# A gated linear-attention layer with a gated MLP: operand loads issued in two halves at two places of the cycle

## The chip, the cores and the metric

The kernel runs on one core of one Trainium2 chip. The metric is the device time of one execution in microseconds (us), lower is better. PE is TensorE with its matmuls, PEld its weight loads, DVE is VectorE, ACT ScalarE, POOL GpSimd, and SP (SPq in rows) the queue that issues every DMA of this kernel.

## The reference

The first half is a recurrence over 768 steps for 4 batches and 8 heads of 40 channels; its output, laid out as 320 channels per step, goes through a gated MLP.

```python
for t in range(S):                       # S = 768
    y[:, :, t] = einsum('bhd,bhde->bhe', r_t, state)
    Sa = einsum('bhde,bhe->bhd', state, a_t)
    state = state * w_t[:, :, None, :] - einsum('bhd,bhe->bhde', Sa, b_t)
    state = state + einsum('bhd,bhe->bhde', v_t, k_t)
x = y.transpose(0, 2, 1, 3).reshape(B, S, 320)
h = gelu_tanh(x @ w_in)                  # 320 -> 1024
u, v = h[..., :512], h[..., 512:]
v_n = (v - mean(v)) / sqrt(var(v) + 1e-6) * g_ln
v_s = einsum('ts,bsd->btd', w_sg, v_n) + b_sg
out = x + (u * v_s) @ w_out
```

## The kernel before, in words

The recurrence is cut into 12 chunks of 64 steps (`NCH`, index `c`), and the 4 batches into two pairs (index `f`). One pass over a chunk for both `f` is called a cycle here. Per `(c, f)` there are two strings of pieces. The *gate* pieces (`gate_1` to `gate_n`) turn the operands w, k, a, b of a chunk into decayed keys (`kb`, transposed to `kbt`) and 64x64 blocks (`ab`); they run several chunks ahead. The *chain* pieces (`chain1` to `chain5` on PE, with their `post` pieces on ACT and DVE) carry the state from chunk to chunk. In between, the inverse of a triangular matrix is built, most of it on POOL (`inv_sub`, tile names `tg` and `x`), and parts of the MLP (`fill_x`, `fill_v`, `fill_out`, tiles `xf`, `hf`, `hv`) are put into the cycles from chunk 2 on. The rest of the MLP follows the attention.

Every piece has a position, a number in units of a plan (one cycle is 25.258 units, `PER`). The pieces are sorted by position and written out in that order, and each engine runs its own instructions in exactly this order. A position is an order, not a time: what stands behind a waiting instruction on the same engine waits too. That holds for SP as well.

The pieces that matter here issue DMAs on SP:

- `load_main` (L274) fills one of two tiles `main` with the operands w, k, a, b of the chunk pair `2c+f+2`, in two DMAs: 40 channel rows into partitions 0 to 39 and 40 rows into partitions 64 to 103. It stands at `y + n[5] + LATE` (L663), behind the second `gate_3`, the last reader of the tile. The next reader is `gate_1` of the following cycle.
- `load_rv` (L492) fills `rts[f]` and `vuts[f]` with r and v for the next chunk in four DMAs, two for each half `x` of the partitions. It stands at `z + n[13] + LATE` (L670), behind `chain5`, and is next read by `chain4` of the following cycle.
- `store5` (L628) writes the chunk's output in four DMAs (`xd<-yt`), `load_vb` (L481) loads v in another layout (`vs<-vb`), `fill_x` loads earlier outputs again (three DMAs, `xf<-xd`), and `fill_out` stores a piece of the MLP (`hd<-hv`).

With the positions of the file, SP meets in a cycle, for `f` = 0 and 1 as marked: `vs` (0), `xf`, `rv` (1), `store5` (1), `hd`, `main` (0), `vs` (1), `xf`, `rv` (0), `main` (1), `store5` (0), `hd`. On PE a cycle is, by tile names: hf, kt, gp, pq, ru, xp, tp, yp, us, hf, ut, ab, kt, ru, pq, us, sp, ut, yp, ab.

Of the kernel before, what the change touches and what calls it, by code (L numbers as in the profile page):

```python
# [16 lines left out]
B, H, S, D = 4, 8, 768, 40  # L17
# [23 lines left out]
LOADS = -12.0  # L41
PER = 25.258
LATE = 2.5
STORE = 1.5
GATE = ((-101.908, -100.107, -99.028, -96.184, -97.801, -95.604, -92.188, -90.251, -93.577, -91.478, -91.823),
    (-93.163, -92.271, -89.673, -85.987, -88.462, -85.151, -80.147, -78.616, -83.325, -79.712, -81.287))
GATE0 = {(0, 0): (-50.0, (0, 0.6, 1.2, 2.0, 2.1, 3.5, 5.0, 6.2, 6.1, 10.6, 7.4)), (0, 1): (-43.168, (-2.368, -1.768,
# [159 lines left out]
def engines(tc):  # L207
    nc = tc.nc
    return tuple(InOrder(tc, e) for e in (nc.vector, nc.scalar, nc.gpsimd, nc.tensor, nc.sync))
# [6 lines left out]
def attention(tc, a, xd, flag, keep, ps, mlp=None):  # L216
# [3 lines left out]
    V, A, G, T, Q = engines(tc)  # L220
    with ExitStack() as ctx:
# [20 lines left out]
        def static(nm, n, shape, where=None):  # L242
            return [(where or st).tile(shape, F32, name=f"{nm}{i}") for i in range(n)]
# [11 lines left out]
        n = WU  # L255
# [7 lines left out]
        rts = static("rt", 2, [128, 2, 4, C])  # L263
        call = keep.tile([128, NCH * B, NP], F32, name="call")
        vuts = static("vut", 2, [128, 2, 2, 4, C])
# [5 lines left out]
        def main_of(i):  # L271
            return mains[i % 2]

        def load_main(i):  # L274
            if i < 2 * NCH:
                for h in range(2):
                    Q.dma_start(out=main_of(i)[64 * h:64 * h + D], in_=a["main"][i, D * h:D * h + D])

        warm = gt.tile([128, 128], F32, name="warm")
        V.memset(warm, 0.0)  # L280
# [208 lines left out]
                A.copy(out=vus[f][0:64, 0:2 * DM].rearrange("p (g h x d) -> p g h x d", g=4, h=2, x=2),  # L489
                       in_=vss[f][0:64].rearrange("p i (g x) h d -> p (i g) h x d", x=2))  # L490

        def load_rv(c, f):  # L492
            if c < NCH:
                for x in range(2):
                    r = slice(64 * x, 64 * x + D)
                    Q.dma_start(out=rts[f][r], in_=a["rt"][c, f, x])
                    Q.dma_start(out=vuts[f][r, 0], in_=a["vt"][c, f, x])

        def chain1(c, f):
            at, vs = at_of(c, f), vss[f]  # L500
# [138 lines left out]
        def at_(p, f, *args, **kw):  # L639
            pieces.append((p, f, args, kw))  # L640
# [4 lines left out]
            at_(ZEROS + 0.01 * k, f)  # L645
        for f in range(2):
            at_(LOADS, load_vb, 0, f)
            at_(LOADS, load_rv, 0, f)
        for c in range(NCH):
            for f in range(2):  # L650
                y, n = GATE0.get((c, f)) or (YG[c], GATE[f])
                at_(y + n[0], gate_1, c, f, 0)
                at_(y + n[1], gate_1, c, f, 1)
                at_(y + n[2], gate_2, c, f, E={"V": V, "G": G}[GATEE.get((c, f), GE)[0]])
                at_(y + n[3], gate_c, c, f)
                for i in range(2):
                    at_(y + n[4 + i], gate_3, c, f, i, E={"V": V, "G": G}[GATEE.get((c, f), GE)[1]])
                for g, p in zip((gate_t, gate_k, gate_s), n[6:]):
                    at_(y + p, g, c, f)
                for h in range(2):  # L660
                    at_(y + n[9] + 0.001 * h, gate_a, c, f, h)
                    at_(y + n[10] + 0.001 * h, gate_n, c, f, h)
                at_(y + n[5] + LATE, load_main, 2 * c + f + 2)  # L663
                z, n = YC[c], CHAIN0.get((c, f), CHAIN[f])
                for g, p in zip((chain1, post1, chain_t, post_t, chain2, post2, chain3, post3, copy3, chain_u, post_u, chain4, post4, chain5, post5), n):
                    at_(z + p, g, c, f)
                at_(z + n[14] + STORE, store5, c, f)
                at_(z + n[0] + LATE, load_vb, c + 1, f)
                at_(z + max(n[6], n[9]) + LATE, load_vu, c + 1, f)
                at_(z + n[13] + LATE, load_rv, c + 1, f)  # L670
            z = YC[c]
            for (g, *k), p in zip(((inv_back, 0), (inv_back, 1), (inv_back, 2), (inv_g,), (post_g,), (inv_x,), (post_x,)), BACK0.get(c, BACK)):
                at_(z + p, g, c, *k)
        for g in GROUPS:
            z, v = (0, INV0[g[0]]) if g[0] in INV0 else (YC[g[0]], INV)
            at_(z + v[0], inv_load, g)
            at_(z + v[1], inv_in, g)
            for s in range(31 - LAST):
                y = {}
# [523 lines left out]
def attention_then_gated_mlp(tc, ins, out):  # L1203
    nc = tc.nc
    a = ins
    with ExitStack() as ctx:
        keep = ctx.enter_context(tc.tile_pool(name="keep", bufs=1))
        dr = ctx.enter_context(tc.tile_pool(name="x_dram", bufs=1, space=bass.MemoryType.DRAM))
        xd = dr.tile([B, DM, S], F32, name="xd")
        flag = keep.tile([1, 1], I32, name="flag")  # L1210
        mlp = [a[k] for k in ("w_in", "w2", "g_ln", "wst", "b_sg", "w_out", "seq_w")]
        ps = Banks(tc, ctx)
        part = Mlp(tc, ps, xd, *mlp, out)
        part.hd = dr.tile([B, LASTF, 128, HF], F32, name="hd")
        verdict = attention(tc, a, xd, flag, keep, ps, part)
        part.run(True, verdict)
        bad = nc.values_load(flag, min_val=0, max_val=1)
        with tc.If(bad > 0):
            sequential(tc, [a["seq_" + k] for k in "rkvwab"], xd)
            Mlp(tc, ps, xd, *mlp, out).run(False)  # L1220
# [60 lines left out]
```

## Time and profile before

| | |
|---|---|
| time, median of 3 runs | 648.37 us (646.72 to 649.48) |
| the profiled execution's own time | 651.27 us |
| its span, first to last instruction | 649.5 us |
| PE / DVE / ACT / POOL busy | 85% / 77% / 56% / 57% of the span |
| mean granted TensorE clock | 0.899 of full speed |
| chain that ended last | PE 46%, DVE 26%, issue 10%, POOL 7%, ACT 6%, DMA 2% |

The profile is one execution; its own time is what the shares and stretches belong to. The chain that ended last is followed back from the last instruction to what released each step. "issue" in it is time in which an engine waited for nothing that the profile shows. [...] DMA shares are of 16 DMA engines.

### The profile page before, as it was taken

The page shows a single profiled execution, that of the slowest core. Times are in us where ns is not written, and L with a number is a line of the kernel's source. Part 1 is how long each engine was busy: PE and PEld are TensorE (multiplying, and loading weights), DVE is VectorE, ACT ScalarE, POOL GpSimd, SP SyncE. Part 2 cuts the span into 40 slices and gives each one's busy share as a digit, 9 for nine tenths or more (in the row PEclk, how much of TensorE's full clock was granted, in tenths as well). Part 3 has the DMA queues.
Part 4 walks back from the last instruction along what each step waited for, and adds up shares of the span by engine and source line. Part 5 has one row for each costly group of instructions (what it writes and reads, how often), then busy time and mean ns, then how long its engine had stood idle before and what let it go on. Part 6 is the DMA issues. An engine that isn't in the chain of part 4 may idle for free.

```text
span 649.5 us, 25246 instructions
## 1 busy us (share of the span) xinstructions
PE 551.1 (85%) x10734; PEld 502.6 (77%) x10734; DVE 496.9 (77%) x954; ACT 363.6 (56%) x769; POOL 370.0 (57%) x600
## 2 busy tenths in 40 slices
PE   6438859768998798999998799698998998899896
PEld 5327758657887787888887687597998987899896
DVE  7767989699779566877799856748699799778943
ACT  3333957457877576787867678556345324625410
POOL 3485838816974844588389642656644632544331
PEclk8658877567999897999998899788999999999999
DMA  5443334243444353553354346337023541401001
GB/s 194 130 120 94 96 80 117 77 121 89 128 113 134 91 151 92 154 131 108 105 137 134 106 133 168 106 113 203 14 80 104 157 144 67 124 26 56 30 13 55
DMA packets 54945, 69.69 MB, mean 107 GB/s; under 512 B 21704, under 2 KB 39752, under 8 KB 52808
## 3 DMA queue, kind: packets, MB, share of 16 engines
q1 hardware_dynamic: 54824, 67.99, 36.8%
q8 instruction: 86, 1.41, 1.0%
q14 instruction: 35, 0.29, 0.1%
HBM read 54.86 MB, written 13.11 MB: 105 GB/s over the span
## 4 chain that ended last, share of the span: by engine, by line
PE 46%; DVE 26%; issue 10%; POOL 7%; ACT 6%; DMA 2%; SPq 1%; DVEq 0%; POOLq 0%; ACTq 0%
PE sg L202 7%; PE yp L202 5%; PE hf L202 4%; PE op L202 3%; DVE v L202 3%; PE sp L202 3%; PE ab L202 3%; PE pq L202 3%; PE ut L202 3%; PE ru L202 3%; DVE stg L202 3%; PE hu L202 3%; PE kt L202 2%; PE xp L202 2%; DVE p L202 2%
## 5 line engine op out<-in xcount | busy, mean ns | idle before, releaser
L202 POOL TENSOR_TENSOR tg<-x,n 128x135 f32<-128x135 f32 (+25 forms) x203 | 106.2, 523 | 98.1 <-ACT gs L202 40.0
L202 POOL TENSOR_TENSOR x<-x,tg 128x135 f32<-128x135 f32 (+25 forms) x203 | 108.2, 533 | 15.9
L202 PE MATMUL sg<-wsh,vh 128*128 128x384 f32 x192 | 65.9, 343 | 4.6 <-DVE y L202 3.9
L202 PE MATMUL sg<-wsh,vl 128*128 128x384 f32 x192 | 66.0, 344 | 3.5 <-POOL vl L202 3.5
L202 PE MATMUL sg<-wsl,vh 128*128 128x384 f32 x192 | 65.8, 343 | 1.7 <-DVE wsl L202 0.9
L202 ACT ACTIVATE nts<-ab 32x512 f32<-32x512 f32 x96 | 46.5, 484 | 28.2 <-PE ab L202 27.0
L202 PE MATMUL kt<-ident,kb 128*128 128x128 f32 x192 | 35.4, 333 | 27.4 <-DVE fixed L202 17.8
L202 POOL TENSOR_TENSOR gx<-g,gy 128x384 fp32r<-128x384 f32 x30 | 32.0, 1076 | 40.1 <-ACT gy L202 40.1
L202 PEld LDWEIGHTS kt<-ident,kb 128*128 128x128 f32 x192 | 26.7, 170 | 32.6 <-issue 26.7
L202 DVE TENSOR_TENSOR at<-ab,mask 64x512 f32<-64x512 f32 x48 | 31.8, 677 | 26.1 <-ACT nts L202 25.4
L202 POOL TENSOR_TENSOR rs<-rs,mhalf 128x1 f32<-128x1 f32 x24 | 14.7, 615 | 64.9 <-DVE rs L202 61.3
L202 ACT CAST vh<-v 128x512 fp32r<-128x512 f32 x24 | 14.6, 620 | 58.3 <-DVE v L202 58.3
L202 PE MATMUL ab<-at,kb 64*64 64x64 f32 x1536 | 39.6, 269 | 7.1 <-DVE fixed L202 6.2
L202 PEld LDWEIGHTS ab<-at,kb 64*64 64x64 f32 x1536 | 35.7, 179 | 10.1 <-issue 8.4
L202 ACT CAST gy<-g 128x384 fp32r<-128x384 f32 x30 | 15.3, 513 | 50.2 <-DVE g L202 50.2
L202 PEld LDWEIGHTS sg<-wsh,vh 128*128 128x128 f32 x192 | 36.5, 190 | 5.9 <-issue 2.6
L202 PEld LDWEIGHTS sg<-wsh,vl 128*128 128x128 f32 x192 | 36.6, 191 | 5.4 <-POOL vl L202 5.4
L202 PE MATMUL yp<-pqs,kbt 128*64 128x64 f32 x768 | 33.5, 249 | 7.8 <-ACT vs L202 3.4
L202 PEld LDWEIGHTS yp<-pqs,kbt 128*64 128x64 f32 x768 | 29.5, 159 | 11.6 <-ACT vs L202 3.6
L202 PEld LDWEIGHTS sg<-wsl,vh 128*128 128x128 f32 x192 | 36.5, 190 | 2.3 <-DVE wsl L202 1.2
L202 PE MATMUL sp<-vu,kbt 128*64 128x40 f32 x704 | 28.1, 237 | 11.6 <-issue 8.7
L202 DVE SCALAR_TENSOR_TENSOR g<-sg,gl,bt 128x384 f32<-128x384 f32 x32 | 19.5, 610 | 23.9 <-POOL gx L202 14.9
(158 smaller groups left out, 1609.2 us busy)
## 6 DMA issues: line engine op xcount, KB each, us to landing
main<-main SPq DMA_DIRECT2D x44, 321.4 KB
hd<-hv SPq DMA_DIRECT2D x20, 256.0 KB
v<-hd SPq DMA_DIRECT2D x20, 256.0 KB
vs<-vb SPq DMA_DIRECT2D x24, 160.0 KB
rt<-rt SPq DMA_DIRECT2D x48, 80.0 KB
vut<-vt SPq DMA_DIRECT2D x48, 80.0 KB
xd<-yt SPq DMA_DIRECT2D x96, 40.0 KB
ws<-seq_w SPq DMA_DIRECT2D x20, 192.0 KB
```

The source lines that it names most:

```text
L202: return self.tc.keep_in_program_order(f(*a, **k))
```

## The change

The two DMAs of `load_main` become two pieces, and the four of `load_rv` become two pieces of two. The first half stays where it was. The second half of `main` moves later by 4.6 units for `f` = 0 and 3.4 for `f` = 1, from chunk `c` = 2 on; the second half of r and v moves later by 1.7 and 1.15 units, for all chunks. Bytes, shapes and number of DMAs stay.

```diff
+MAIN_GAP = (4.6, 3.4)
+RV_GAP = (1.7, 1.15)
...
-        def load_main(i):
+        def load_main(i, h):
             if i < 2 * NCH:
-                for h in range(2):
-                    Q.dma_start(out=main_of(i)[64 * h:64 * h + D], in_=a["main"][i, D * h:D * h + D])
+                Q.dma_start(out=main_of(i)[64 * h:64 * h + D], in_=a["main"][i, D * h:D * h + D])
...
-        def load_rv(c, f):
+        def load_rv(c, f, x):
             if c < NCH:
-                for x in range(2):
-                    r = slice(64 * x, 64 * x + D)
-                    Q.dma_start(out=rts[f][r], in_=a["rt"][c, f, x])
-                    Q.dma_start(out=vuts[f][r, 0], in_=a["vt"][c, f, x])
+                r = slice(64 * x, 64 * x + D)
+                Q.dma_start(out=rts[f][r], in_=a["rt"][c, f, x])
+                Q.dma_start(out=vuts[f][r, 0], in_=a["vt"][c, f, x])
...
-            at_(LOADS, load_rv, 0, f)
+            for x in range(2):
+                at_(LOADS, load_rv, 0, f, x)
...
-                at_(y + n[5] + LATE, load_main, 2 * c + f + 2)
+                for h in range(2):
+                    at_(y + n[5] + LATE + (MAIN_GAP[f] if h and c > 1 else 0), load_main, 2 * c + f + 2, h)
...
-                at_(z + n[13] + LATE, load_rv, c + 1, f)
+                for x in range(2):
+                    at_(z + n[13] + LATE + (RV_GAP[f] if x else 0), load_rv, c + 1, f, x)
```

## Rows read from the trace of the kernel before

**Rows 1.** The page, parts 1, 3 and 6: engines, queues, DMA issues.

```profile
PE 551.1 (85%) x10734; PEld 502.6 (77%) x10734; DVE 496.9 (77%) x954; ACT 363.6 (56%) x769; POOL 370.0 (57%) x600
...
q8 instruction: 86, 1.41, 1.0%
...
main<-main SPq DMA_DIRECT2D x44, 321.4 KB
```

**Rows 2.** Busy time by stretch: us, engines, granted clock, DMA share, GB/s.

```profile
90.00:115.00 25.00, 21.01 (x602) 19.17 (x603) 24.55 (x44) 15.95 (x36) 18.33 (x33) 0.69 0.42 111
...
156.60:221.40 64.80, 57.52 (x1891) 51.49 (x1883) 51.11 (x95) 50.03 (x109) 49.27 (x85) 1.00 0.49 129
221.40:228.20 6.80, 6.60 (x161) 6.29 (x161) 2.36 (x5) 1.31 (x2) 6.09 (x10) 0.50 0.05 14
...
252.20:259.00 6.80, 6.80 (x163) 6.42 (x162) 4.38 (x12) 2.35 (x5) 0.00 (x0) 0.50 0.06 18
```

**Rows 3.** The chain that ended last: start us, us, what.

```profile
115.13 1.52 issue
...
168.02 2.05 PE hf L202 x8
...
191.25 1.08 PE ut L202 x32
192.32 1.67 PE yp L202 x64
...
194.93 2.05 PE hf L202 x8
...
200.08 1.88 issue
...
217.82 3.78 issue
...
221.93 1.90 PE ut L202 x32
223.83 2.93 PE yp L202 x64
...
228.43 2.05 PE hf L202 x8
...
248.17 2.54 issue
...
258.83 2.14 PE hf L202 x8
...
276.74 1.09 PE pq L202 x64
```

**Rows 4.** Timeline of SP, 195 to 260 us: start us, us, what.

```profile
195.54 0.66 SPq L202 DMA_DIRECT2D main<-main  x2
...
212.96 0.71 SPq L202 DMA_DIRECT2D main<-main  x2
213.84 0.48 SPq L202 DMA_DIRECT2D vs<-vb  x1
...
228.30 0.66 SPq L202 DMA_DIRECT2D main<-main  x2
...
242.88 0.71 SPq L202 DMA_DIRECT2D main<-main  x2
...
245.81 0.47 SPq L202 DMA_DIRECT2D vs<-vb  x1
...
257.15 0.29 SPq L202 DMA_DIRECT2D rt<-rt  x1
```

**Rows 5.** Busy time in a stretch with little but one `main` pair moving.

```profile
157.50:161.50 4.00, 4.00 (x147) 3.72 (x144) 3.01 (x7) 3.74 (x9) 3.61 (x6) 1.00 0.54 150
```

**Rows 6.** Timeline of DVE, 240 to 242.5 us: the next reader of a `main` tile.

```profile
241.44 1.27 DVE L202 TENSOR_TENSOR_SCAN ex<-main,fixed 128x260 f32<-128x260 f32 x2
```

**Rows 7.** Timeline of POOL, 150 to 430 us; in brackets idle time before, and releaser.

```profile
264.89 0.24 POOL L202 TENSOR_TENSOR tg<-x,n 128x31 f32<-128x31 f32 x1 [12.80 <-ACT gs L202]
```

## The prediction

> **What bounds the kernel now.** I read the busy time by stretch first, then the chain that ended last, then the SP timeline beside both. From about 156 to 286 us the chain is an almost unbroken string of PE matmuls, so what PE loses there the kernel loses. A cycle from `hf` to `hf` takes 26.91 us (168.02 to 194.93), then 33.50 (to 228.43), then 30.40 (to 258.83) [rows 3]. The two long cycles hold the two longest "issue" pieces, 3.78 us at 217.82 and 2.54 us at 248.17, in which PE waited for nothing that the profile names [rows 3]. Behind each, the granted clock is 0.50 for 6.80 us, while it was 1.00 from 156.6 to 221.4, through the shorter stop of 1.88 us at 200.08 [rows 2, 3].
>
> What is PE waiting for? The page has a queue of kind "instruction" with 86 packets in 1.41 MB, 16.4 KB each; PE and PEld have 21,468 instructions, 250 for each packet [rows 1]. So I take these packets for PE's program, and a stop without a releaser for a packet that came late. The stops follow the `main` pairs: 212.96 and 217.82 (4.9 us later), 242.88 and 248.17 (5.3), 195.54 and 200.08 (4.5) [rows 3, 4]. A pair is 2 x 321.4 = 643 KB [rows 1]; where hardly anything else moved, the rate was 150 GB/s [rows 5], so a pair drains in about 4.29 us and a half in 2.14, an estimate. My reading: a program packet asked for while a pair is in the DMA queues comes only behind all of it.
>
> [...]
>
> **The change part by part.** No DMA is added and none gets smaller, so SP's issue time stays. What changes is what SP has between two halves.
>
> *Second half of main, f = 0.* The position moves by 4.6 units past one piece, `load_vb` of f = 1, and stays ahead of `fill_x`. A position alone makes no pause; `vs` does, since it waits for PE's `ru`. After the pair at 242.88, `vs` went out at 245.81, so the second half comes about 3.4 us behind the first, past the 2.14 us that the first needs. After the pair at 212.96, `vs` went out at 213.84, so the second half comes at about 214.4, only 1.4 us behind the first [rows 4]. There a packet gets between the halves only if it was asked for in that time. Queued behind the moved half is `xf`, as before.
>
> In both cycles I take it that the packet now waits for one half, not two. The stop of 3.78 becomes 3.78 - 2.14 = 1.64 us and that of 2.54 becomes 0.40. Both are shorter than the 1.88 us after which the clock stayed at 1.00 [rows 2, 3], so the half-clock stretches go too. Their price: `ut` took 1.90 us instead of 1.08 and `yp` 2.93 instead of 1.67 [rows 3], 1.755 times as long. PE's 6.60 busy us in the first stretch [rows 2] are then 3.76 at full clock, 2.84 lost; the 6.80 of the second are 3.87, 2.93 lost. Gains: 2.14 + 2.84 = 4.98 and 2.14 + 2.93 = 5.07, together 10.05 us. The other way round: the two cycles are longer than the one at 168.02 by 6.59 and 3.49, together 10.08, which that sum may take but hardly exceed unless the common cycle shortens as well.
>
> *Second half of main, f = 1.* It moves by 3.4 units behind the four stores, the second r and v piece and `hd`. It then drains in the stretch gp, pq, ru, xp, tp, yp, where PE uses instructions fastest: `pq`, 64 matmuls and 64 loads, takes 1.09 us [rows 3], so a packet of 250 lasts 2.13 us there. A half of 2.14 us in the way is as long as that whole packet. For the first half the same sum as above applies: the stop of 1.88 at 200.08 may go. Between a gain of 1.88 and a loss of 2.14 for each of the five or so cycles from 156 to 286, I take nothing, and keep -1.9 and +10.7 as the ends.
>
> *Is the later half still in time?* The tightest pair I found is that at 228.30, whose reader starts at 241.44 [rows 4, 6]: 13.1 us, less 4.3 for the drain of both, leaves 8.8. The new place costs three to four, so nothing. If the cover were gone, `gate_1` would wait on DVE, with `pqs` and `yt` behind it, and PE for those.
>
> *Second half of r and v.* It moves behind the four stores of the same f, which wait for DVE's `yt`. The first half goes out at 257.15, `pq` reads it at 276.74 [rows 3, 4]: 19.6 us cover some three of delay. Stores go out a little earlier, and the burst ahead of the f = 1 pair is smaller by half. I take nothing, with ends of -1 and +1 us.
>
> *Before 156 us.* From 90 to 115 us DVE is busy for 24.55 of 25 us [rows 2], so PE's stops are mostly covered; the one at 115.13, on the chain, has 1.52 us [rows 3]. I take nothing and keep -1.5 as an end.
>
> *Where the time goes next.* If PE runs ahead, POOL's inverse could become late. But POOL sat idle for 12.80 us before 264.89, waiting for ACT's `gs` behind a PE product [rows 7], more than the sum of 10.05. So the rest moves forward with PE.
>
> **The sum.** Against the profiled execution: 651.27 - 10.05 = 641.2. It is 2.90 above the median of 648.37. Were the 2.90 in these very stops, the gain on the median would be 7.2; were they elsewhere, 10.05. I go halfway: 648.37 - 10.05 + 1.45 = 639.8 us.
>
> **The rivals.**
>
> *One stop goes, the other stays.* The pause after the pair at 212.96 is only 1.4 us [rows 4], and a packet that comes after it waits for both halves as now. For it: that narrow gap. Against it: the longer stop is also the one with most to lose. Time: 648.4 - 5.0 = 643.4.
>
> *The queue is not the cause.* If the program packets take turns with the data, or the stops have some other cause that the profile does not name, smaller bursts change nothing: 648.4. For it: the profile shows no releaser, and the `main` pair at 228.30 has no long stop within six us. Against it: both long stops come at the same distance behind f = 0 pairs. [...]
>
> *The second halves make stops of their own.* The f = 1 half drains where a packet lasts 2.13 us of PE time, so a packet behind it stops PE for up to 2.14; the stop of 2.54 [rows 3] was followed by the half clock, at 2.9 us each time. One such stop costs about 5.0; two eat the gain of 10.05, and from the third the kernel is slower: 648.4 - 10.05 + 15.1 = 653.5. For it: place and rate. Against it: the halves leave pauses that the pair did not, and total bytes are the same.
>
> **How the numbers follow.** Both stops fall: 0.58, with its own range 634 to 643. The low end is where the stop at 200.08 (1.88), that at 115.13 (1.52) and some of the smaller ones go too. One falls: 0.19. Nothing changes: 0.13. New stops win: 0.10. The prediction is that of the first. The range from 633 to 647.5 takes in the first two cases and the near edge of the third; it leaves out the rest of the third, all of the fourth and a small tail below. 0.5% is 3.2 us, near the 2.8 us that the three runs spread over: faster than 645.1 in the first two cases, 0.77; within 0.5% 0.14; slower 0.09.
>
> **What would show it.** In the changed profile, SP's timeline should have `vs` between the two f = 0 halves, and stores, r and v, and `hd` between those of f = 1. The "issue" pieces near `sp` should be under 2 us and the granted clock 1.00 from 156 to the last `main` load. The `hf` to `hf` cycles should all be near 27 us. DVE's scans should still wait for no `main` load but the first. The prediction is wrong if "issue" pieces of over 2 us stand in gp to yp behind a second half, if `sp` still stops for over 2.5 us, or if the cycles are even but the end does not move, POOL or DVE having taken over.

## Result and the profile after

The changed kernel took 642.84 us in the median (634.84 to 655.75, 20 runs), the kernel before 649.53 us on the same chip (644.52 to 656.08, 20 runs). The ratio is 0.9867 with an interval of 0.9837 to 0.9897: faster by 1.3%, about 8.6 us. This ratio is taken over the fast runs alone, 11 of the 20 of the changed kernel; the medians of all runs are 6.7 us apart, a ratio of 0.9897. The forecast was 639.8 against 648.37, a ratio of 0.9868. A second measurement of the same kernel gave 0.9892 [0.985, 0.9934].

Single executions scatter by 12 us (before) and 21 us (changed), so what one profile gained is not the gain of the median. Two executions of the changed kernel were profiled. The rows below are of the one of 638.85 us, with a span of 637.1, beside 651.27 and 649.5 before; it is the fastest of the six runs of the second measurement. Where the other one, of 645.22 us, differs is said further down. The busy time of PE, first line of the page of the changed kernel, fell by 8.1 us with the same 10734 matmuls [rows 1]: the same work ran at a higher mean granted clock, 0.916 of full speed, not 0.899.

```profile
PE 543.0 (85%) x10734; PEld 494.3 (78%) x10734; DVE 496.4 (78%) x954; ACT 363.0 (57%) x769; POOL 368.9 (58%) x600
```

The chain that ended last, changed kernel: start us, us, what.

```profile
160.72 2.05 PE hf L204 x8
...
187.54 2.05 PE hf L204 x8
...
192.66 1.91 issue
...
211.80 1.25 issue
...
213.25 1.08 PE ut L204 x32
214.33 1.67 PE yp L204 x64
...
217.27 2.05 PE hf L204 x8
...
236.73 0.23 issue
236.96 1.59 PE sp L204 x46
238.55 1.08 PE ut L204 x32
239.63 1.54 PE yp L204 x50
241.17 0.34 issue
...
242.87 2.04 PE hf L204 x8
```

Read it against [rows 3]. Three cycles took 82.15 us (160.72 to 242.87), not 90.81 (168.02 to 258.83). The stop in `sp` of 3.78 us is 1.25, that of 2.54 is 0.23 with 0.34 more in `yp`. Behind them `ut` takes 1.08 and `yp` 1.67 us again, where they took 1.90 and 2.93. The third stop, in `pq`, is as it was: 1.91, before 1.88. The cycles are 26.82, 29.73 and 25.60 us, so the second is not near 27, as the prediction wanted it.

This sums up. Less stop: 3.78 - 1.25 = 2.53 and 2.54 - 0.57 = 1.97. No half clock behind them: 2.84 and 2.93 us by the prediction's working. Against this a new stretch at the lower clock behind the stop at 192.66, the second row here (columns as in [rows 2]):

```profile
100.00:156.00 56.00, 41.44 (x1221) 37.31 (x1215) 53.24 (x105) 36.58 (x85) 38.29 (x64) 0.82 0.42 111
...
195.50:199.00 3.50, 3.50 (x85) 3.36 (x82) 3.40 (x8) 1.51 (x4) 2.87 (x6) 0.53 0.35 97
```

PE was busy for 3.50 us there, 1.99 at full clock by the factor 1.755, so 1.5 us lost. 2.53 + 1.97 + 2.84 + 2.93 - 1.5 = 8.8 us; measured 8.66.

In the execution of 645.22 us the same three cycles took 86.37 us (165.86 to 252.23), 4.44 less than before. Both stops in `sp` are short, but behind the first `ut` runs at the lower clock (0.53 on average from 219 to 226 us; behind the second 1.00, from 246.9 to 250.4):

```profile
217.28 1.51 issue
...
219.02 1.90 PE ut L204 x32
...
245.36 1.60 issue
...
248.55 1.08 PE ut L204 x32
```

So shorter stops are common to both executions; a full clock behind both is not.

The row from 100 to 156 us belongs to a gain that the prediction did not have: the stretch of PE work begins 7.30 us earlier (160.72, not 168.02). The same stretch of the kernel before has a lower clock, 0.65, and less done, 1023 matmuls instead of 1221:

```profile
100.00:156.00 56.00, 42.98 (x1023) 38.52 (x1022) 48.50 (x100) 32.25 (x70) 33.37 (x57) 0.65 0.38 101
```

In the execution of 645.22 us the stretch of PE work begins only 2.2 us earlier (165.86). So at 242.87 the execution of the rows above is 16.0 us ahead, and its span is 12.4 shorter (637.1 against 649.5); 3.6 us are given back behind that point.

The timeline of SP, changed kernel, shows the pauses between two halves: start us, us, what.

```profile
205.68 1.29 SPq L204 DMA_DIRECT2D main<-main  x1
207.84 0.47 SPq L204 DMA_DIRECT2D vs<-vb  x1
208.36 0.51 SPq L204 DMA_DIRECT2D main<-main  x1
...
216.79 0.28 SPq L204 DMA_DIRECT2D main<-main  x1
217.16 1.61 SPq L204 DMA_DIRECT2D xd<-yt  x4
...
221.57 0.28 SPq L204 DMA_DIRECT2D main<-main  x1
...
231.49 0.30 SPq L204 DMA_DIRECT2D main<-main  x1
234.38 0.47 SPq L204 DMA_DIRECT2D vs<-vb  x1
234.90 0.98 SPq L204 DMA_DIRECT2D main<-main  x1
```

For f = 0 the second half follows 2.7 and 3.4 us behind the first, with `vs` between them; for f = 1 4.8 us, with the stores and the rest between them.

The cover held. All that DVE waited for on `main` is the first load of the kernel (view of the tile `main`, changed kernel: releaser, us, times), and POOL still sits idle 8.39 us at the place that had 12.80 [rows 7]:

```profile
  DMA main<-first: 1.7, 1
```

```profile
249.66 0.24 POOL L204 TENSOR_TENSOR tg<-x,n 128x31 f32<-128x31 f32 x1 [8.39 <-ACT gs L204]
```

### The profile page after: what moved, and what is told of

Same layout as the page of the kernel before. It is cut to its first block, busy times and chain, and to the rows that moved or that the text cites. A ratio compares the mean times of both kernels' runs of the same rounds, so it can differ in the third digit from the quotient of the medians.

```text
span 643.5 us, 25238 instructions
## 1 busy us (share of the span) xinstructions
PE 554.0 (86%) x10734; PEld 506.0 (79%) x10734; DVE 498.1 (77%) x954; ACT 363.6 (56%) x769; POOL 369.4 (57%) x600
## 4 chain that ended last, share of the span: by engine, by line
PE 57%; DVE 21%; issue 6%; ACT 6%; POOL 6%; DMA 1%; SPq 1%; ACTq 0%; DVEq 0%; POOLq 0%
PE sg L204 10%; PE yp L204 6%; PE hf L204 5%; PE op L204 4%; PE sp L204 4%; PE ut L204 4%; PE ru L204 3%; PE ab L204 3%; PE kt L204 3%; PE pq L204 3%; DVE v L204 3%; PE hu L204 3%; PE xp L204 3%; PE us L204 2%; DVE p L204 2%
## 5 line engine op out<-in xcount | busy, mean ns | idle before, releaser
L204 PE MATMUL pq<-rt,vut 40*64 40x64 f32 x1536 | 32.2, 229 | 5.2 <-issue 4.2
L204 DVE TENSOR_TENSOR pqs<-pq,mask 128x512 f32<-128x512 f32 x48 | 30.7, 679 | 7.7 <-PE pq L204 7.7
## 6 DMA issues: line engine op xcount, KB each, us to landing
main<-main SPq DMA_DIRECT2D x44, 321.4 KB
hd<-hv SPq DMA_DIRECT2D x20, 256.0 KB
v<-hd SPq DMA_DIRECT2D x20, 256.0 KB
```

The lines of the kernel that those rows point to most:

```text
L204: return self.tc.keep_in_program_order(f(*a, **k))
```

## Experiments

Theory: PE's stops without a releaser are program packets that come late behind a burst of loads; shorter bursts shorten them. Rivals: the gain is from the later place, from one half alone, or from r and v; or the queue has no part in it. The interval of a ratio is that against the kernel before on the same chip.

**Only the main loads in two halves.**

```
-RV_GAP = (1.7, 1.15)
+RV_GAP = (0, 0)
```

> Only main in two halves; r and v in one piece as before. Theory (PE's program packets wait behind the main pair in the DMA queues): all of the gain stays, ratio to before about 0.987, and the stop in sp near 217 us is about 1.5 us long, not 3.8. Rival (the stores that go out earlier and the smaller r and v burst give the gain): ratio about 1.00 and the stop near 3.8 us.

Measured: 0.9939 [0.990, 0.9978], 645.65 us. The stops in `sp` were 0.42 and 0.29 us, the three cycles 83.10. The same kernel once more:

> Main in halves alone, a second time. If it repeats 0.994 while the whole change stays at 0.987 to 0.989, r and v in two pieces add some 0.5% on top of main, though alone they gave nothing. If it comes out at 0.988 to 0.990, the first difference was scatter between runs.

Measured: 0.9883 [0.9827, 0.994], 643.13 us; three cycles 82.35. So `main` alone gives most or all of the gain. By the medians of all runs (645.65 and 643.13 against 651.99 and 651.74) it is 0.9903 and 0.9868, beside 0.9897 for the whole change.

**Only r and v in two halves.**

```
-MAIN_GAP = (4.6, 3.4)
+MAIN_GAP = (0, 0)
```

> Only r and v in two pieces; main in one pair as before. Theory: nothing, ratio 0.998 to 1.002, with stops of about 3.8 us near 217 us and 2.5 us near 248 us as before. Rival (the r and v part gives the gain): ratio about 0.987.

Measured: 1.0013 [0.9969, 1.0057]. Its three cycles took 91.31 us, with stops of 1.79 and 2.86 in `sp`. It gave nothing that can be measured. That the first of these stops is 1.79 us behind an undivided pair, and 4.36 in the run with f = 1 halves below, shows how far one stop differs between executions.

**Only the f = 0 halves.**

```
-MAIN_GAP = (4.6, 3.4)
-RV_GAP = (1.7, 1.15)
+MAIN_GAP = (4.6, 0)
+RV_GAP = (0, 0)
```

> Only the main pair of f = 0 in two halves, that of f = 1 and r and v as before. Theory: the two long stops in sp stand behind f = 0 pairs, so nearly all of the gain is here, ratio about 0.988. Rival (each pair gives a share): ratio about 0.993, half of it.

The chain, and below it the busy time by stretch just behind its stop at 199.32:

```profile
167.46 2.06 PE hf L204 x8
...
199.32 1.91 issue
...
217.04 0.80 issue
...
241.74 0.57 issue
...
248.23 2.05 PE hf L204 x8
```

```profile
202.50:206.00 3.50, 3.50 (x124) 3.18 (x123) 3.24 (x7) 2.00 (x4) 3.03 (x7) 1.00 0.32 95
```

Three cycles took 80.77 us, 10.04 less than before: the two terms of the prediction, which were to be 10.05, appear with the f = 0 halves alone. Just behind these cycles PE stopped for another 1.89 us at 254.45, with the lower clock behind it: `yp` took 2.67 us, not 1.67. The stretch begins at 167.46, as before (168.02). Yet the timed ratio is 1.0012 [0.9968, 1.0055]. The profiled execution, 643.71 us, is the fastest of its twelve runs; their median is 648.64 against 651.99, 3.35 us less. So 10 us are not in the typical run.

**Only the f = 1 halves.**

```
-MAIN_GAP = (4.6, 3.4)
-RV_GAP = (1.7, 1.15)
+MAIN_GAP = (0, 3.4)
+RV_GAP = (0, 0)
```

> Only the main pair of f = 1 in two halves. Theory: the long stops in sp stay (3.8 and 2.5 us), the stops in pq and xp behind the f = 1 pairs change by under 2 us in either direction, ratio 0.997 to 1.003. Rival (each pair gives a share): ratio about 0.993. Rival of the prediction (the f = 1 half makes stops of its own in gp to yp): ratio 1.003 or more.

The chain:

```profile
160.63 2.06 PE hf L204 x8
...
209.25 4.36 issue
...
213.82 1.90 PE ut L204 x32
...
239.91 2.54 issue
...
250.66 2.05 PE hf L204 x8
```

The mirror image: both `sp` stops are there with the half clock behind (`ut` 1.90), three cycles take 90.03 us; but the stretch begins at 160.63, 7.4 us early. The timed ratio is 0.9950 [0.9909, 0.9992], the medians 648.50 against 651.99.

What was won early shows in the chain of this kernel, then of the one before, at the same work:

```profile
112.13 1.17 PE sp L204 x31
...
115.39 1.08 PE ut L204 x32
```

```profile
116.64 1.40 PE sp L202 x21
...
121.81 1.90 PE ut L202 x32
```

Before, PE stands on the chain here at half clock behind the stop of 1.52 us at 115.13 [rows 3]; with the f = 1 halves there is no stop and full clock. With the f = 0 halves alone the stop is gone from here too, but `sp` still takes 1.90 us for 32 matmuls, the lower clock.

**Both halves at the later place.** The pair as long as before, moved as a whole.

```
-RV_GAP = (1.7, 1.15)
+RV_GAP = (0, 0)
...
-at_(y + n[5] + LATE + (MAIN_GAP[f] if h and c > 1 else 0), load_main, 2 * c + f + 2, h)
+at_(y + n[5] + LATE + (MAIN_GAP[f] if c > 1 else 0), load_main, 2 * c + f + 2, h)
```

> The main pair stays one burst, but as a whole it stands where the change puts its second half; r and v as before. Theory (the length of the burst counts): a packet that meets the pair still waits for all of it, ratio 0.997 to 1.01, with stops of over 2 us somewhere between 156 and 286 us. Rival (the later place counts, not the splitting): ratio about 0.994, as with main in halves.

Measured: 1.0030 [0.9987, 1.0073]. The place alone gives nothing. SP's timeline, then the chain, show the stop moving with the pair:

```profile
246.32 0.47 SPq L204 DMA_DIRECT2D vs<-vb  x1
246.88 0.84 SPq L204 DMA_DIRECT2D main<-main  x2
```

```profile
251.43 1.54 PE yp L204 x50
252.97 2.58 issue
```

It comes 6.1 us behind the pair, no longer 18 matmuls into `sp` but 50 into `yp`. The changed kernel's chain shows both places in one cycle, with 46 + 32 + 50 = 128 matmuls between the stop at 236.73 and that at 241.17. With a weight load each that is 256 instructions. In the kernel before, 22 program packets start from 156.36 us until the next one at 256.83, and PE has 2804 matmuls and 2800 loads in that stretch, 127 of each for a packet. So I take it that the stops fall where a packet begins, and that a late burst hits the next packet: place and count agree in it, where the prediction had only the count of 250 [rows 1].

**A burst half as long again.** The kernel before with a third load of 321.4 KB behind each pair from the seventh on, into a tile that nobody reads.

```
+if i > 5:
+    Q.dma_start(out=extra[0:D], in_=a["main"][i, 0:D])
...
+extra = gt.tile([128, ML], F32, name="extra")
```

> The kernel before, with a third DMA of the same 321.4 KB behind each main pair (into a tile that nobody reads) from tile 6 on. Theory (a program packet waits behind all that is queued): each stop behind a pair grows by up to 2.1 us, 217 to nearly 6 us and 248 to nearly 4.7, more stops reach 2 us, more half-clock stretches; ratio 1.01 to 1.03. Rival (the stops are not the queue): stops as before, ratio 1.00.

Measured: 1.0275 [1.0234, 1.0315], 668.47 us. The chain:

```profile
205.71 3.27 issue
...
227.26 4.90 issue
...
232.39 1.90 PE ut L202 x32
...
258.92 3.08 issue
```

At the same places before: 1.88, 3.78 and 2.54 us [rows 3]. All grew, by 0.5 to 1.4, under the 2.14 us in which the added load drains by the prediction's estimate; the lower clock follows all three (behind the first `ru` took 1.86 us, not 1.06; behind the second the granted clock was 0.52 on average from 228 to 238 us, behind the third 0.54 from 263 to 270), and the three cycles take 100.98 us. A burst makes these stops, and no reader of its data is there to blame.

**40 rows as 32 and 8.** Before, and then the changed kernel, each load as two, of 32 and 8 rows, one right behind the other.

```
-Q.dma_start(out=main_of(i)[64 * h:64 * h + D], in_=a["main"][i, D * h:D * h + D])
+for lo, hi in ((0, 32), (32, D)):
+    Q.dma_start(out=main_of(i)[64 * h + lo:64 * h + hi], in_=a["main"][i, D * h + lo:D * h + hi])
```

> The kernel before with each 40-row DMA of main issued as 32 rows and 8 rows, at the same place and with the same bytes. [...] Rival (total bytes count, not rows on an engine): ratio 1.00 to 1.003, for two more issues on SP.

> The changed kernel with each 40-row half issued as 32 and 8 rows. [...] Rival (spreading the rows gave 0.997 alone, so it gives nothing here): ratio 0.987 to 0.991, two more issues on SP included.

Measured: 0.9974 [0.9932, 1.0016] on the kernel before, 0.9884 [0.9821, 0.9948] on the changed one. The second ratio rests on 3 of 12 runs; the medians are 650.05 against 651.74, a ratio of 0.9974, so it stays open whether the pieces cost the changed kernel its gain. On the kernel before, one stop in `sp` fell to 1.01 us and the other grew to 3.08. There more pieces without a pause between them do nothing that can be measured. Why 32 and 8 rows should help was the author's estimate: to which engines of the DMA the rows go no row here shows.

**The changed kernel once more**, beside these:

> The changed kernel itself, beside the others. If r and v add nothing on top of main, it repeats main alone, ratio 0.994; if the two parts add up to more than each alone, it repeats its own first ratio, 0.987.

Measured: 0.9892 [0.985, 0.9934].

**Four quarters.** 20 rows each, at four positions.

```
-MAIN_GAP = (4.6, 3.4)
+MAIN_GAP = ((0, 4.6, 6.5, 10.2), (0, 1.38, 3.4, 8.4))
...
+p, r = 64 * (h // 2) + 20 * (h % 2), 20 * h
+Q.dma_start(out=main_of(i)[p:p + 20], in_=a["main"][i, r:r + 20])
```

> The changed kernel with main in four DMAs of 20 rows: f = 0 with one before vs, one behind vs, one behind xf, one behind the next r and v; f = 1 with one before the stores, one behind them, one behind hd, one behind the next vs. Theory: a packet waits for 1.1 us at most, stops near 217 and 248 us under 1 us, no half clock between 156 and 280; ratio 0.980 to 0.987. Rival (with halves the rate at which packets come is the limit, not the queue): ratio 0.987 as with halves.

Measured: 1.0080 [1.0052, 1.0107], 655.42 us. One stop in `sp` is down to 0.30 us, at 222.28, and that of the next cycle is gone, but the loads now cost something themselves. SP's timeline and DVE's, early in the kernel:

```profile
58.89 1.41 SPq L204 DMA_DIRECT2D main<-main  x4
```

```profile
64.55 1.28 DVE L204 TENSOR_TENSOR_SCAN ex<-main,fixed 128x260 f32<-128x260 f32 x2 [5.07 <-DMA main<-main]
```

By the positions of the file, the last f = 0 quarter is the third of these four. It stands behind the first pieces of the next tile, and these wait for that tile's last reader until 58.89; the three earlier quarters went out by 47.55. DVE's scan waits for it; in the changed kernel the same scan starts at 59.57. Later the chain leaves PE:

```profile
252.79 1.67 SPq L204
...
255.70 2.88 DMA xd<-yt
258.58 0.57 ACT gs L204
```

By SP's timeline the piece at 252.79 is two quarters being issued, ahead of the four stores that the chain goes on through. So with more pieces SP's own order is late next.

**f = 0 in three pieces** of 20, 20 and 40 rows, in the later cycles only.

```
+MAIN_GAP4 = (0, 4.6, 6.5, 6.5)
...
+for h in range(4 if c > 4 and f == 0 else 2):
+    if c > 4 and f == 0:
+        at_(y + n[5] + LATE + MAIN_GAP4[h], load_main4, 2 * c + f + 2, h)
```

> The changed kernel with the f = 0 load of main in pieces of 20, 20 and 40 rows from c = 5 on: before vs, behind vs, behind xf. Theory: the stops in sp fall from 1.3 to 1.6 us to under 0.6 us as with quarters, and nothing is late, since the early chunks keep their halves; ratio 0.983 to 0.987. Rival (what quarters lost came from the pieces themselves, by more issues on SP and later loads): ratio 0.99 or more.

Measured: 0.9918 [0.9879, 0.9958], 645.68 us. The stops on its chain are 1.71, 1.13 and 0.32; the chain runs through `xd` stores and `gs` in this kernel too, 3.45 us in one such store. No version tried is better than the changed kernel by more than the intervals.

## Why the prediction was right, and where it was not

**The cause.** Longer burst, longer stops, slower; halves with a pause, shorter stops; an undivided pair moved, the stop moves and nothing is gained. The traces also keep every single DMA packet, which no view above lists, and there the late thing itself can be seen. From 100 to 300 us the fourteen traces hold 129 stops of PE of over 0.3 us without a releaser. Each of them ends 1.0 to 1.7 us after a packet of 16,384 bytes of the instruction queue has landed. Six of them, in us; a row of `main` is one packet of 8,228 bytes, and a pair has 80:

| stop | kernel | the 128 matmuls before it begin | program packet, start to landing | rows of the burst started before it | PE goes on |
|---|---|---|---|---|---|
| 3.78 | before | 214.3 | 218.84 to 220.10 | 80 of 80 | 221.60 |
| 2.54 | before | 245.2 | 247.77 to 249.20 | 80 of 80 | 250.70 |
| 1.88 | before | 197.3 | 199.33 to 200.49 | 53 of 80 | 201.96 |
| 1.25 | changed | 208.2 | 210.10 to 211.51 | 40 of 80 | 213.05 |
| 4.90 | burst half as long again | 223.8 | 229.61 to 230.88 | 120 of 120 | 232.16 |
| 3.08 | burst half as long again | 256.0 | 259.21 to 260.47 | 88 of 120 | 262.00 |

So PE's program is late, and it is late in starting: once started, a packet takes 0.9 to 1.8 us in the kernel before, with or without a stop. Behind both long stops it started after the last row of the pair; in the changed kernel it went between the halves. "Only behind all of it", as the prediction reads it, is too strong: at 199.33 it started after 53 of 80 rows. The rival "the queue is not the cause" falls.

A part of every stop is not the queue's. In the kernel before, from 156 to 262 us, a packet started only 0.2 to 2.6 us after PE had begun the block before it (4.6 before the stop of 3.78), so here the program comes about one block ahead. At these 129 stops 2.2 to 3.5 us passed from the start of a packet until PE went on, and 128 matmuls at the pace of `pq` take 2.2 us. So small stops stay, of 0.30 us even with four quarters.

In which order the engines of the DMA serve the two queues no row here shows, so whether program packets take turns with the data, as that rival had it, the traces neither bear out nor refute; against the rest of it speak a longer burst (1.0275) and halves (0.9867), which did change the time. Why the packet starts behind 80 rows in one case and 53 in another stays open.

**The f = 0 term.** Predicted 1.64 and 0.40 us for the stops, found 1.25 and 0.57 in one execution, with the half clock behind them gone, and 1.51 and 1.60 in the other, with the half clock behind the first still there. 10.05 predicted, 10.04 with these halves alone, in the profiled executions; so near a match is luck, as the stops were 0.80 and 0.57 there. The drain was taken too short: 4.2 to 4.8 us for the seven pairs before from 156 to 250 us, not 4.29, and 2.3 to 3.5 for a half in the changed kernel, not 2.14. One slip adds to this: the page's KB are 1,024 bytes (40 rows of 8,228 bytes are its 321.4 KB), so that 643 KB at 150 GB/s are 4.39 us. The first pause was 2.7 us, not 1.4, since `vs` went out 2.2 us behind the first half, not 0.9; the rival that one stop stays rested on that gap, and no stop of the old length stayed in either execution.

**The f = 1 term.** Nothing inside the three cycles, as taken: 90.03 against 90.81 us. The stop in `pq` did not move, and none of over 2 us came up behind a second half; the rival of new stops is out.

**The step that failed: "Before 156 us", where PE's stops were taken as covered by DVE**, at 0 with an end of -1.5. DVE's 24.55 of 25 us were read as cover, but they end at 115; just behind, PE itself is on the chain for 10 us at a granted clock of 0.50. The start of the stretch came 7.3 us early in this execution and 7.4 with the f = 1 halves alone; 3.8 and 1.9 with `main` only. With f = 0 alone it was 0.6. But the other execution of the changed kernel began only 2.2 early, and the kernel before with 32 and 8 rows 3.4, so part of this is scatter between executions.

**The clock.** "Stops shorter than 1.88 leave it at 1.00" was one case read as a rule. Behind the stop of 1.91 at 192.66 the granted clock fell to 0.53 for some 3.4 us; behind the one of 1.91 at 199.32, f = 0 alone, it was 1.00. Behind stops of 1.08 us (both loads later, at 204.53) and 1.13 (three pieces, at 211.10) it fell too, to 0.66 and 0.69 over the 3.5 us from half a microsecond behind the stop. So the length of a stop does not decide it alone, and the sign "1.00 from 156 to the last `main` load" did not come.

**The total.** The ratio of 0.9867 met the forecast's 0.9868, but so close a match is luck: the medians of all runs give 0.9897, 6.7 us of the 8.6 that were forecast. In the profiled execution the gain also came by terms that were not those of the sum: an early gain that it lacked, and 3.6 us given back behind 243 us that it did not foresee. The 3.0 us between 639.8 and 642.84 hold 1.2 of a slower median before (649.53, not 648.37). How the gain is shared between the two halves stays open. By the ratios, 1.0012 for f = 0 and 0.9950 for f = 1, they do not add up to the whole; by the medians each gives about the same, 0.9949 and 0.9946, and their product of 0.9895 is that of the whole, 0.9897.

**r and v.** Nothing that can be measured, as taken: 1.0013 alone, while `main` alone gave 0.9939 and 0.9883 and the whole change 0.9867 and 0.9892. The first of each stand just outside each other's intervals (from 0.990, and up to 0.9897); the repeats do not bear a difference out.

## What to carry to other kernels

An idle engine for which the profile names no releaser, a few us behind a large burst of loads, may be waiting for its own program: count the instructions between two such stops (here 128 matmuls with 128 loads), and look for a packet of the instruction queue that lands just before the engine goes on (here 1.0 to 1.7 us before). Break the burst with a real pause, as a piece that waits on the queue makes it (`vs`, 2.7 and 3.4 us; 32 and 8 rows with no pause gave 0.9974), and test by lengthening the burst as well as by cutting it. Don't put the last piece behind an instruction that waits, nor ahead of stores that others wait for (four quarters, 1.0080).

## What the runs showed of the hardware

- A stop of PE can cost more than itself: behind those of 2.54 to 4.90 us the granted clock was lower. Behind the two of the kernel before it was 0.50 for 6.80 us each [rows 2], `ut` took 1.90 instead of 1.08 us, and some 2.9 us more were lost each time by the prediction's working. Stops of 1.1 to 1.9 us went both ways: 0.53 behind one of 1.91 us, 1.00 behind another.
- Loads that nobody reads slowed the kernel by 2.75%, with DMA busy for less than half of the time in the PE stretch before, 0.49 [rows 2].
- The stops of PE lie 128 matmuls with 128 weight loads apart, or a multiple of that less a few, counted in the traces of six kernels, and so at the same places of the program in each: 63 matmuls into one `sp`, 18 into the next, 57 to 59 into `pq`. Which of them is long goes with the load ahead of it: by the table above all 80 rows had started before the packets of the stops of 3.78 and 2.54 us, 53 before that of 1.88, and 40 before that of 1.25.
